# Decoding the second part's weights earlier, by way of DRAM, in a mixer and two-layer MoE kernel

## The chip, the cores and the metric

One core of a Trainium2 chip runs the whole program. The metric is device time in microseconds. The kernel before takes 967.74 us (median of 3 runs, 966.28 to 967.86). Engines are named as in the profile: PE (TensorE), DVE (VectorE), ACT (ScalarE), POOL (GpSimd), SP (the queue that issues most DMAs).

## What is computed

A linear-attention recurrence, then two feed-forward blocks on its output of 3072 rows of 384:

```
for t in range(768):                                  # 4 x 8 heads, 48 wide
    y[t] = r[t] @ (state + (u * k[t]) v[t]^T);  state = w[t] * state + k[t] v[t]^T
x = y, heads side by side                             # 3072 x 384
x = (sigmoid(x @ w_gate) * (x @ w_val)) @ w_out       # hidden 1536
h = x @ w_in                                          # hidden 2048
out = (h * tanh(log(1 + exp(h)))) @ w_out2
```

All of it is float32. The products of the feed-forward blocks are made on PE from pairs of float16 numbers (a high half and the rest), three products for each.

## The kernel before

**Pairs.** The 768 steps are cut into 24 chunks j of 32 steps, and these into 12 pairs p (0 to 11). Of each pair, `fine(p)` (L465) makes the scores inside a chunk: products on POOL into tiles `pt` and updates of the loaded block `blk` (L486), sums of `pt` on DVE into `A` (L506). `coarse(p)` (L563) turns them into operands for PE: DVE flips `RD`, `KD`, `WD` and `X`, PE makes the scores `lp` (L638), ACT and DVE merge them into `X` (L655), and three steps `scaled` (L623) multiply parts of `RD`; the last of these (768 elements) follows `lp` and stands before `yp`. `keys(p)` makes `KT` and, on ACT, `KK` (L697). `step(j)` (L706) makes the chunk's output `yp` (L728), the state's outer product `kp` (L824), its decay (L804) and its sum (L835). The output leaves as `xs` (L212, L215) and comes back transposed as `xt` by a transposing DMA that ACT issues (L762).

**First block.** For each pair 12 units `gate(p, f)` (L857): products `gv` on PE (L880), then sigmoid, product and two halves `gt` on ACT and DVE (L891 to L911). Their second product `out1(p - 1, c, part)` (L932) adds up in PSUM as `o` (L944), goes through `xo` (L212, L215) and is stored in DRAM as `x2d` (L980).

**Second block.** It begins when all pairs are done: `h_unit` (L1039) makes `h` on PE (L1054) from the weights `wis`, `operands` (L1071) sums on POOL (L1088) and halves on DVE and ACT, `out2` (L1135) multiplies by the weights `wps` (L1169). The seven products of `out2` need sums of weight blocks.

**Weights.** All weights come as 64-bit words, and are decoded to two float16 halves (`decode`, L271): a load `raw` (SP, L267), two steps on ACT (`word` L248, `low` L238), a joining step on DVE (`word`, L292), the high half (L303) and the rest (L306). For `wps`, `combine` (L314) takes the place of the last two: differences `sum_wp` (L332), then three high halves (L346) and three rests (L332). In the kernel before the second block's weights are decoded straight into `wis` and `wps`. That space is free once the attention is done (`open_a`, L1029, and `open_b`, L1035), so the 16 decodings are listed in `tail_end` (L1284), which is called at gate 7 of pair 10. Engines are given as prices: `W2HI` lets ACT or DVE make the high half, `W2LO` POOL or DVE the rest.

**Order.** Every step is a task with an engine (or several with a price each), a cost, what it reads and writes, and `lat`, the time after its end at which a follower counts as ready (`SEM`, 0.1, if nothing is said). `Plan.run` (L96) gives each task the latest time at which it may stand, from its followers, and then lists the tasks: at each step the engine that is free first takes, of the tasks that are ready, the one with the earliest latest time. PE's tasks keep their latest times in the order in which they were added. All engines then run their lists in order, SP's queue too. So a changed cost or `lat` can move any instruction.

Of the kernel before, what the change touches and what calls it, by code (L numbers as in the profile page):

```python
# [19 lines left out]
NP = NJ // 2  # L20
# [19 lines left out]
NPT = 32  # L40
NRAW = 1
YPOS = (4, 7)
SEM = 0.1
SHARED = (0,)
WHOLE = range(1, 12, 2)
COLD = 1.9
# [113 lines left out]
def mixer_moe_kernel(  # L160
# [100 lines left out]

    def load_raw(key, pool, src, n, slot, reads=()):
# [6 lines left out]
        add("sp", 2.2, go, reads, [("raw", slot)], lat=2.0)  # L269

    def decode(key, dst, n, count, slot, reads, high_on, lo_on, halves=False, blocks=None):  # L271

# [37 lines left out]
        full = 1.15 if key[0] == "wo" else 0.95  # L310
        add("act", 0.78, rebase, [raw, "consts", "table1"], [word])
        add("act", 1.1, bits3, [raw, "consts"], [low])
        add("dve", full, join, [low], [word])
        if halves:  # L314
            combine(key, dst, word, low, reads, high_on, lo_on, count)
            return
        made = [[(key[0], f, a) for f in blocks or [key[1]]] for a in range(2)]
        add(high_on, 0, high, [word, *reads], made[0])
        add(lo_on, 0, rest, [word, *made[0]], made[1])

    def combine(key, dst, word, low, reads, high_on, lo_on, count):
        sums = {}
# [28 lines left out]

        add({"pool": 1.8, "dve": 1.1}, 0, differ, [word], [low])
        for n, part in ((0, 0.25), (1, 0.5), (2, 1.0)):
            src = low if n == 2 else word
            cost = {e: c * part + 0.1 for e, c in high_on.items()}
            add(cost, 0, lambda e, n=n: high(e, n), [src, *reads], [(*key, 0, n)])
            cost = {e: c * part + 0.1 for e, c in lo_on.items()}
            add(cost, 0, lambda e, n=n: rest(e, n), [src, (*key, 0, n)], [(*key, 1, n)])

# [128 lines left out]
    def fine(p):  # L488
# [377 lines left out]
    def gate(p, f):  # L866
# [61 lines left out]
        else:  # L928
            add("act", 0.34, high, [ps], [(*G, 0), *room])
        add("dve", 0.35, rest, [ps, (*G, 0)], [(*G, 1)])  # L930
# [63 lines left out]
    def open_a(e):  # L994

        sf.close()
        w2["i"] = sb.enter_context(tc.tile_pool(name="w2i", bufs=1))
        w2["wi"] = w2["i"].tile([128, 2, KC, F2], F16, name="wis")

    def open_b(e):  # L1000
        sa.close()
        w2["p"] = sb.enter_context(tc.tile_pool(name="w2p", bufs=1, side="right"))
        w2["raw"] = sb.enter_context(tc.tile_pool(name="raw", bufs=1, side="right"))
        w2["ph"] = sb.enter_context(tc.tile_pool(name="ph", bufs=1, space=PS, side="right"))
        w2["po"] = sb.enter_context(tc.tile_pool(name="po2", bufs=1, space=PS, side="right"))
        w2["wp"] = w2["p"].tile([128, 2, 7, NF2 // 2, HD], F16, name="wps")
        w2["h"] = sb.enter_context(tc.tile_pool(name="hp", bufs=1, side="right"))

    homes = []
# [31 lines left out]
    def h_unit(r, f):  # L1041
# [3 lines left out]
        E = ("e", k)  # L1045
        fs = slice(128 * f, 128 * f + 128)

        def sums(e):
# [3 lines left out]
            for a, c in ((0, 0), (0, 1), (1, 0)):  # L1052
                for kc in range(KC):
                    nc.tensor.matmul(  # L1054
                        hps[r, f],
                        w2["wi"][:, a, kc, fs],
                        x2[r][:, c, kc, :],
# [8 lines left out]

        w = [("wi", f // 2, a) for a in range(2)]
        add("pe", 1.95, sums, [*w, ("x2", r % 2)], [ps])
# [75 lines left out]
    def out2(r, m, h):  # L1144
# [13 lines left out]
        def sums(e):  # L1158
# [8 lines left out]
            for i in range(NF2 // 2):  # L1167
                for a, c in ((0, 0), (1, 0), (0, 1)):
                    nc.tensor.matmul(  # L1169
                        ops2[h, first],  # L1170
                        home(slots[r, i, name])[:, c, tsl],
                        w2["wp"][:, a, w, i, :],
                        start=(new and n == 0),
# [22 lines left out]
        if m == 0 and h == 0:  # L1196
            add("none", 0, start, [], [O])
        n = {0: 0, 1: 1, 2: 1}.get(w, 2)
        reads = [("slot", slots[r, i, name], c) for i in range(NF2 // 2) for c in range(2)]
        reads += [("wp", i, a, n) for i in range(NF2 // 2) for a in range(2)]  # L1200
        add("pe", 1.95, sums, reads, [bank])
# [82 lines left out]
    def tail_end():  # L1284
# [3 lines left out]
        for i in range(8):  # L1288
            cs = slice(256 * i, 256 * i + 256)
            dst = lambda cs=cs: w2["wi"][:, :, :, cs]  # L1290
            load_raw(("wi", i), lambda: dp, in_cols(wi, cs), (KC, 256), i % 3)
            decode(("wi", i), dst, (KC, 256), i, i % 3, ["opened"], W2HI, W2LO)
        add("none", 0, open_b, [], ["attention", "open"])
        for i in range(8):
            cs = slice(2 * i, 2 * i + 2)
            dst = lambda i=i: w2["wp"][:, :, :, i]
            slot = (i + 2) % (3 + NRAW)
            pool = (lambda: dp) if slot < 3 else (lambda: w2["raw"])
            reads = [] if slot < 3 else ["open"]
            load_raw(("wp", i), pool, in_rows(wo2, cs), (2, DM), slot, reads)  # L1300
            decode(("wp", i), dst, (2, DM), i, slot, ["open"], W2HI, W2LO, True)

# [4 lines left out]
    for p in range(NP):  # L1307
        for f in range(NF1):
# [94 lines left out]
```

## Time and profile before

| | us |
|---|---|
| median of 3 runs | 967.74 |
| the profiled execution, its own time | 966.43 |
| its span, first to last instruction | 964.7 |
| PE busy | 895.7 |
| DVE busy | 663.6 |
| ACT busy | 496.4 |
| POOL busy | 490.7 |

The program has four stretches: a start in which the weights of the first block are decoded (0 to 160 us), the steady pairs (to about 500), a change-over in which the last pairs run while the second block's weights are decoded (to about 595), and the second block. An engine's busy time within a stretch, beside the stretch's length, tells whether it is the limit there. Idle time of PE is then looked up by what ended it.

### The profile page before, as it was taken

The numbers are of one execution on the slowest core, as the hardware profiler recorded it, in microseconds if no ns is written. First come the engines' busy times: TensorE is split into PE (matmuls) and PEld (weight loads), VectorE is DVE, ScalarE is ACT, GpSimd is POOL, SyncE is SP. The second block draws the span as 40 slices with busy tenths as digits, with TensorE's granted clock in tenths as the row PEclk, the third lists the DMA queues.
The fourth block names the chain that finished last, engine by engine and source line by source line (L and its number), as shares of the span: only waits on it lengthen the run. The fifth ranks groups of instructions, "written<-read, shape, count | busy, mean of one in ns | idle before, by whom it ended". The sixth has DMA issues, their size and how long they took to land.

```text
span 964.7 us, 29601 instructions
## 1 busy us (share of the span) xinstructions
PE 895.7 (93%) x12808; PEld 715.9 (74%) x12808; DVE 663.6 (69%) x1202; ACT 496.4 (51%) x1191; POOL 490.7 (51%) x534
## 2 busy tenths in 40 slices
PE   0667899999999999999999889999999999999998
PEld 0455678888888888888888777657767676776788
DVE  7889976767676757686778798875565655556541
ACT  2757864343525344343536566775565655656540
POOL 7999832626464545546364365654343443444330
PEclk9988899999999999999999999999999999999999
DMA  9445832322232323133223760010100102000000
GB/s 307 152 139 163 265 115 75 65 67 72 68 57 72 83 62 76 50 75 71 60 41 101 169 204 12 8 43 1 38 30 10 58 1 66 2 9 26 1 34 34
DMA packets 56467, 71.92 MB, mean 75 GB/s; under 512 B 20752, under 2 KB 37648, under 8 KB 56208
## 3 DMA queue, kind: packets, MB, share of 16 engines
q1 hardware_dynamic: 39696, 66.09, 23.6%
q10 hardware_dynamic: 16640, 3.94, 2.1%
q8 instruction: 100, 1.64, 0.7%
q14 instruction: 31, 0.25, 0.1%
HBM read 56.64 MB, written 9.44 MB: 68 GB/s over the span
## 4 chain that ended last, share of the span: by engine, by line
PE 72%; DVE 13%; ACT 7%; POOL 3%; issue 2%; ACTq 2%; DMA 1%; SPq 0%; DVEq 0%; POOLq 0%
PE gv L880 20%; PE h L1054 19%; PE o L1169 17%; PE o L944 10%; PE yp L728 3%; ACT X L655 2%; ACTq L762 2%; ACT KK L697 2%; DVE X L655 1%; DVE A L506 1%; PE lp L638 1%; POOL pt L486 1%; DVE gt L911 1%; PE kp L824 1%; DVE s L835 1%
## 5 line engine op out<-in xcount | busy, mean ns | idle before, releaser
L1054 PE MATMUL h<-x,wis 128*128 128x512 f16 x864 | 199.9, 379 | 0.0
L486 POOL TENSOR_TENSOR blk<-blk 128x384 f32<-128x384 f32 (+2 forms) x139 | 129.4, 943 | 97.6 <-DMA blk<-rkw 69.9
L880 PE MATMUL gv<-xt,wgs 128*128 128x256 f16 x1296 | 165.9, 278 | 12.3 <-DVE gt L911 11.9
L944 PE MATMUL o<-gt,wos 128*128 128x256 f16 x1296 | 165.2, 273 | 5.9 <-DVE xo L215 5.9
L1088 POOL TENSOR_TENSOR sum<-e 128x256 f32<-128x256 f32 x96 | 71.5, 744 | 186.3 <-ACT e L1065 186.2
L880 PE MATMUL gv<-xt,wvs 128*128 128x256 f16 x1296 | 163.6, 276 | 2.5 <-DVE wvs L306 1.2
L880 PEld LDWEIGHTS <-wgs 128*128 128x128 f16 x1296 | 126.3, 100 | 31.4 <-issue 12.9
L1054 PEld LDWEIGHTS <-wis 128*128 128x128 f16 x864 | 83.5, 98 | 82.9
L944 PEld LDWEIGHTS <-wos 128*128 128x128 f16 x1296 | 126.0, 98 | 24.5 <-issue 6.8
L880 PEld LDWEIGHTS <-wvs 128*128 128x128 f16 x1296 | 125.0, 99 | 20.9 <-DVE wvs L306 1.5
L486 POOL TENSOR_TENSOR pt<-blk 128x384 f32<-128x384 f32 x93 | 105.4, 1157 | 47.0 <-DMA blk<-rkw 43.6
L891 ACT ACTIVATE sig<-gv 128x256 f32<-128x256 f32 x144 | 53.5, 385 | 118.2 <-PE gv L880 114.3
L1065 ACT ACTIVATE e<-h 128x512 f32<-128x512 f32 x96 | 57.2, 596 | 84.6 <-PE h L1054 83.7
L911 DVE TENSOR_TENSOR gt<-gv,gt 128x256 f16<-128x256 f32 x144 | 58.8, 417 | 51.6 <-ACT gt L908 50.1
L908 ACT CAST gt<-gv 128x256 f16<-128x256 f32 x144 | 52.6, 371 | 75.9 <-DVE gv L896 55.3
L896 DVE SCALAR_TENSOR_TENSOR gv<-gv,sig 128x256 f32<-128x256 f32 x144 | 60.7, 431 | 29.3 <-ACT sig L891 28.8
L1169 PE MATMUL o<-wps,gt 128*128 128x192 f16 x612 | 74.0, 246 | 0.0
L655 ACT COPY X<-lp 24x64 f32<-24x64 f32 x174 | 44.5, 256 | 38.2 <-DVE X L655 28.1
L1107 DVE SCALAR_TENSOR_TENSOR gt<-e,gt 128x256 f16<-128x256 f32 x41 | 27.3, 675 | 49.6 <-ACT gt L1102 49.6
L506 DVE TENSOR_REDUCE A<-pt 128x32 f32<-128x768 f32 (+1 forms) x60 | 51.4, 863 | 12.3 <-POOL pt L486 12.3
L1169 PE MATMUL o<-wps,wgs 128*128 128x192 f16 x498 | 59.4, 246 | 0.0
L1169 PE MATMUL o<-wps,wos 128*128 128x192 f16 x456 | 57.1, 246 | 0.0
(106 smaller groups left out, 1508.4 us busy)
## 6 DMA issues: line engine op xcount, KB each, us to landing
v<-vt SPq DMA_DIRECT2D x96, 96.0 KB, 3.3
blk<-rkw SPq DMA_DIRECT2D x22, 384.0 KB, 3.5
raw_wi<-wi SPq DMA_DIRECT2D x8, 768.0 KB, 4.8
raw_wp<-wo SPq DMA_DIRECT2D x8, 768.0 KB, 6.2
blk<-rkw SPq DMA_DIRECT2D x11, 512.0 KB, 4.0
raw_wg<-wg SPq DMA_DIRECT2D x6, 768.0 KB, 6.2
raw_wv<-wv SPq DMA_DIRECT2D x6, 768.0 KB, 6.1
raw_wo<-wo SPq DMA_DIRECT2D x6, 768.0 KB, 4.7
```

The source lines that it names most:

```text
L486: engines[e].tensor_tensor(out=pv, in0=a, in1=b, op=ALU.mult)
L506: nc.vector.tensor_reduce(out=cell(), in_=shape(pts.pop(n)), op=ALU.add, axis=AX.X)
L655: put(out=xp[p][rs, xs, t:], in_=lps[p, e][rs, :, c : c + C - t])
L880: nc.tensor.matmul(gps[p, f][:, o], w[:, a, kc, fs], xt[p][:, c, kc, :], start=(n == 0), stop=(n == 3 * KC - 1),)
L891: nc.scalar.activation(out=sgs[p, f], in_=gps[p, f][:, 0], func=AF.Sigmoid, scale=1.0 / (SW * SX))
L896: nc.vector.scalar_tensor_tensor(out=gps[p, f][:, 1], in0=gps[p, f][:, 1], scalar=SG / (SW * SX), in1=sgs.pop((p, f)), op0=ALU.mult, op1=A ...
L911: nc.vector.tensor_tensor(out=gt[p][:, 1, f], in0=gps[p, f][:, 1], in1=gt[p][:, 0, f], op=ALU.subtract,)
L944: nc.tensor.matmul(ops[p, c][:, :NT], wos[:, a, f, cs], gt[p][:, g, f, :], start=(f == 0 and n == 0), stop=(f == NF1 - 1 and n == 2),)
L1054: nc.tensor.matmul(hps[r, f], w2["wi"][:, a, kc, fs], x2[r][:, c, kc, :], start=(n == 0), stop=(n == 3 * KC - 1),)
L1065: nc.scalar.activation(out=es[r, f], in_=hps[r, f], func=AF.Mish, scale=ih)
L1088: engines[e].tensor_tensor(out=sums[0][:, n - 1], in0=a(), in1=b(), op=op)
L1169: nc.tensor.matmul(ops2[h, first], home(slots[r, i, name])[:, c, tsl], w2["wp"][:, a, w, i, :], start=(new and n == 0), stop=(n == 3 * NF2 ...
```

## The change

**Decoding ahead.** `decode_ahead` is new. It decodes one of the 16 pieces (8 of `wi`, 8 of `wp`) into a staging tile in the first block's own buffer `raw2`, and stores it in DRAM (`wid`, `wpd`). `ahead(n, tick)` lists it after gate unit f of pair p where 12 (p - 3) + f = 5 n + 2, that is from pair 3 gate 2 to pair 9 gate 5; its load reads that gate's "tick". Its tasks have `lat` 3.0 (`SLACK`) in place of 0.1, its load 9.0. High halves are ACT's alone, rests and differences POOL's alone. `tail_end` now holds only loads of finished weights from DRAM (`fetch`), 8 of 384 KB into `wis` and 8 of 672 KB into `wps`, whose layouts have the piece as the first index after the partition.

**Planner.** The scores' products of pairs 3 and later have `lat` 1.5 (`EASY`) and the step that multiplies by `U` is priced 1.7 in place of 1.2.

**PSUM.** `out1` of pairs 10 and 11 takes banks "po2" and "po" in turn; before, only pair 11's second one had "po2".

```
-W2HI = {"act": 0.83, "dve": 0.7}
-W2LO = {"pool": 1.65, "dve": 0.92}
+W2HI = {"act": 0.83}
+W2LO = {"pool": 1.65}
...
+    wid = dram.tile([8, 128, 2, KC, 256], F16, name="wid")
+    wpd = dram.tile([8, 128, 2, 7, HD], F16, name="wpd")
...
-        add({"pool": 1.8, "dve": 1.1}, 0, differ, [word], [low])
+        add("pool", 2.4, differ, [word], [low], lat)
...
+    def decode_ahead(name, i, src, n, made, store, tick):
+        key = (name, i)
+        count = 8 * (name == "wp") + i
+        slot = count % 2
+        stage = ("raw", 2)
...
+        add("none", 0, new, [], [stage])
+        load_raw(key, lambda: dp, src, n, slot, [tick], 3 * SLACK)
+        decode(
+            key, lambda: tiles[0], n, count, slot, [stage], W2HI, W2LO, name == "wp", None, SLACK
+        )
...
+        add(
+            "sp",
+            0.6,
+            lambda e: nc.sync.dma_start(out=store[i], in_=tiles[0]),
+            [*parts, stage],
+            [(name, "stored", i)],
+            lat=2.0,
+        )
...
-            attn(both, 0, go, [R, K], [pt])
+            wait = SEM if p < 3 else EASY
+            attn(both, 0, go, [R, K], [pt], wait)
             if scaled:
-                attn("dve", 1.2, times_u, ["U"], [pt])
+                attn("dve", 1.7, times_u, ["U"], [pt])
...
-        last = p == NP - 1
-        bank = "po2" if last and c == 1 else "po"
+        bank = "po2" if p > NP - 3 and (KC * p + c) % 2 else "po"
...
+    def fetch(name, src, i, opened):
+        def go(e):
+            nc.sync.dma_start(out=w2[name][:, i], in_=src[i])
+        made = [(name, i)]
+        add("sp", 0.6, go, [(name, "stored", i), opened], made, lat=2.5)
...
         for i in range(8):
-            cs = slice(256 * i, 256 * i + 256)
-            dst = lambda cs=cs: w2["wi"][:, :, :, cs]
-            load_raw(("wi", i), lambda: dp, in_cols(wi, cs), (KC, 256), i % 3)
-            decode(("wi", i), dst, (KC, 256), i, i % 3, ["opened"], W2HI, W2LO)
+            fetch("wi", wid, i, "opened")
         add("none", 0, open_b, [], ["attention", "open"])
         for i in range(8):
+            fetch("wp", wpd, i, "open")
...
+            n, rem = divmod(NF1 * (p - AHEAD) + f, 5)
+            if rem == 2 and 0 <= n < 16:
+                ahead(n, ("tick", p, f))
```

The order of PE is the same from pair 3 on but for a few units that change places with a neighbour. Three places show what moved. The first is DVE while PE works at gates 1 to 4 of pair 11 (`gv11_1` to `gv11_4`; `xo` is what PE's `o` waits for). Before:

```order
L911 TENSOR_TENSOR gt11_9399<-gv11_2_9404,gt11_9399 128x256
L292 SCALAR_TENSOR_TENSOR word_wp4_9365<-word_wp4_9365,low_wp4_9442 128x768
L346 CAST wps_9219<-word_wp4_9365 128x192
L346 CAST wps_9219<-word_wp4_9365 128x2x192
L896 SCALAR_TENSOR_TENSOR gv11_3_9444<-gv11_3_9444,sig_9501 128x256
L215 SCALAR_TENSOR_TENSOR xo_9515<-o110_0_9389,xo_9515 128x256
L332 TENSOR_TENSOR wps_9219<-word_wp4_9365,wps_9219 128x2x192
L292 SCALAR_TENSOR_TENSOR word_wp5_9498<-word_wp5_9498,low_wp5_9520 128x768
L911 TENSOR_TENSOR gt11_9399<-gv11_3_9444,gt11_9399 128x256
```

The same gates on DVE after the change:

```order
L953 TENSOR_TENSOR gt11_9525<-gv11_2_9531,gt11_9525 128x256
L938 SCALAR_TENSOR_TENSOR gv11_3_9561<-gv11_3_9561,sig_9603 128x256
L953 TENSOR_TENSOR gt11_9525<-gv11_3_9561,gt11_9525 128x256
L219 SCALAR_TENSOR_TENSOR xo_9617<-o110_0_9515,xo_9617 128x256
L938 SCALAR_TENSOR_TENSOR gv11_4_9606<-gv11_4_9606,sig_9650 128x256
```

No decoding is left on DVE there; its last joining step stands in pair 10's first gate. The second place is POOL in the steady pairs, where the block of pair 7 comes in. Before:

```order
L623 TENSOR_TENSOR RD6_4452<-RD6_4452,WD6_4478 128x32x16
L486 TENSOR_TENSOR blk6_2990<-blk6_2990 128x2x8x24
L804 TENSOR_TENSOR s13_4379<-s12_4187,WD6_4478 128x384
L486 TENSOR_TENSOR blk6_2990<-blk6_2990 128x24
L486 TENSOR_TENSOR blk6_2990<-blk6_2990 128x16x24
L486 TENSOR_TENSOR pt_4659<-blk7_3831 128x768
L486 TENSOR_TENSOR pt_4689<-blk7_3831 128x384
L486 TENSOR_TENSOR blk7_3831<-blk7_3831 128x16x24 x2
```

The same place on POOL after the change (`made_wi3` is a rest; `RD6` of 32x24 is the last `scaled`, on which `yp` waits):

```order
L527 TENSOR_TENSOR blk6_3022<-blk6_3022 128x16x24
L846 TENSOR_TENSOR s13_4391<-s12_4191,WD6_4493 128x384
L527 TENSOR_TENSOR pt_4722<-blk7_3851 128x768
L527 TENSOR_TENSOR pt_4745<-blk7_3851 128x384
L310 TENSOR_TENSOR made_wi3_4585<-word_wi3_4461,made_wi3_4585 128x768
L665 TENSOR_TENSOR RD6_4465<-RD6_4465,WD6_4493 128x32x24
L527 TENSOR_TENSOR blk7_3851<-blk7_3851 128x16x24 x2
L527 TENSOR_TENSOR pt_5120<-blk7_3851 128x8x48 x2
```

The last `scaled` has come over from DVE (in pairs 4 to 8 and 10; in pair 11 it went from POOL to DVE), behind a rest. The third place is SP's queue at the change-over. Before:

```order
L980 DMA x2d_86<-xo_8520 128x512
L267 DMA raw_wi5_8645<-wi 128x3x512
L267 DMA raw_wi6_8674<-wi 128x3x512
L980 DMA x2d_86<-xo_8747 128x512
L267 DMA raw_wi7_8804<-wi 128x3x512
L267 DMA raw_wp0_8926<-wo2 128x2x768
L267 DMA raw_wp2_8994<-wo2 128x2x768
L267 DMA raw_wp3_9026<-wo2 128x2x768
L267 DMA raw_wp4_9122<-wo2 128x2x768
```

SP's queue at the change-over after the change:

```order
L395 DMA wpd_88<-made_wp6_8590 128x2688
L1051 DMA wis_8843<-wid_87 128x1536 x8
L1021 DMA x2d_86<-xo_8976 128x512
L1021 DMA x2d_86<-xo_9290 128x512
L395 DMA wpd_88<-made_wp7_8856 128x2688
L1080 DMA x2_0_9369<-x2d_86 128x3x256 x4
L1080 DMA x2_1_9401<-x2d_86 128x3x256 x4
L1051 DMA wps_9365<-wpd_88 128x2688 x7
```

The eight loads of raw words have become one run of eight loads of `wis` and, behind the loads of `x2`, one of `wps`.

## Rows read from the trace of the kernel before

**Rows 1.** The page: busy time, share of the span and instructions of each engine.
```profile
PE 895.7 (93%) x12808; PEld 715.9 (74%) x12808; DVE 663.6 (69%) x1202; ACT 496.4 (51%) x1191; POOL 490.7 (51%) x534
```

**Rows 2.** Stretches: length; busy PE, PEld, DVE, ACT, POOL; clock, DMA share, GB/s.
```profile
60.00:160.00 100.00, 82.78 (x1559) 68.38 (x1557) 83.63 (x145) 72.44 (x153) 65.64 (x58) 0.90 0.51 158
160.00:500.00 340.00, 336.69 (x6574) 290.87 (x6572) 239.24 (x453) 140.15 (x399) 177.49 (x185) 1.00 0.28 66
...
520.00:590.00 70.00, 62.24 (x943) 53.44 (x941) 59.26 (x101) 44.63 (x90) 37.61 (x36) 1.00 0.60 163
590.00:930.00 340.00, 340.00 (x2684) 237.03 (x2683) 206.35 (x395) 197.65 (x461) 148.62 (x193) 1.00 0.07 23
```

**Rows 3.** Waits of PE from 500 to 600: us in total, times, longest.
```profile
PE o L944 <- DVE xo L215: 4.3, 3, 2.3
PE gv L880 <- issue: 1.6, 2, 1.2
PE yp L728 <- issue: 1.4, 2, 0.7
PE yp L728 <- DVE s L835: 0.5, 2, 0.3
```

**Rows 4.** Stretches between PE's four waits on "issue", columns as in rows 2.
```profile
528.45:533.55 5.10, 3.91 (x128) 3.10 (x128) 4.19 (x10) 4.01 (x11) 0.90 (x1) 1.00 0.49 153
533.55:540.75 7.20, 6.00 (x126) 4.79 (x127) 7.17 (x9) 4.16 (x7) 2.39 (x2) 1.00 0.87 173
540.75:545.88 5.13, 4.70 (x128) 3.90 (x128) 4.10 (x5) 3.57 (x8) 1.64 (x1) 1.00 0.94 259
```

**Rows 5.** The page: the queue that brings PE's instructions; packets, MB, share.
```profile
q8 instruction: 100, 1.64, 0.7%
```

**Rows 6.** The page: DMA issues, with count, KB each and us to landing.
```profile
blk<-rkw SPq DMA_DIRECT2D x22, 384.0 KB, 3.5
raw_wi<-wi SPq DMA_DIRECT2D x8, 768.0 KB, 4.8
```

**Rows 7.** Waits of PE from 160 to 500, columns as in rows 3.
```profile
PE yp L728 <- DVE RD L623: 1.8, 3, 0.7
PE yp L728 <- DVE s L835: 1.3, 4, 0.6
```

**Rows 8.** DVE's joining steps from 510 to 592: busy us, mean ns, idle before.
```profile
L292 DVE SCALAR_TENSOR_TENSOR word_wp<-word_wp,low_wp 128x768 uint32<-128x768 uint32 x8 | 8.4, 1047 | 0.9 <-ACT low_wp L238 0.9
```

**Rows 9.** POOL's groups from 510 to 592, columns as in rows 8.
```profile
L332 POOL TENSOR_TENSOR sum_wp<-word_wp,sum_wp 128x192 f32<-128x192 f32 x14 | 10.5, 753 | 1.1
L306 POOL TENSOR_TENSOR wis<-word_wi,wis 128x768 f16<-128x768 f32 x6 | 10.1, 1684 | 19.8 <-DVE wis L303 14.7 <-ACT wis L303 5.1
L332 POOL TENSOR_TENSOR sum_wp<-word_wp 128x384 f32<-128x384 f32 x8 | 8.9, 1116 | 13.1 <-DVE word_wp L292 13.1
L332 POOL TENSOR_TENSOR wps<-sum_wp,wps 128x768 f16<-128x768 f32 x3 | 5.5, 1818 | 0.9 <-ACT wps L346 0.9
...
L623 POOL TENSOR_TENSOR RD<-RD,WD 128x768 f32<-128x768 f32 x1 | 1.5, 1486 | 0.5 <-PE lp L638 0.5
```

**Rows 10.** Line L623 on DVE, 200 to 500: ns min/median/max, first and last start.
```profile
L623 DVE TENSOR_TENSOR RD<-RD,WD x7: 946/949/1597, 217.9 to 482.3; 128x768 f32<-128x768 f32 x7
```

**Rows 11.** PE in order of time, from a pair's last `lp` to `yp`: start, us.
```profile
215.91 0.88 PE L638 MATMUL lp<-RD,KD 64*32 64x48 f32 x64
216.73 2.14 PE L880 MATMUL gv<-xt,wvs 128*128 128x256 f16 x18
...
218.95 0.29 PE L728 MATMUL yp<-s,RD 64*32 64x48 f32 x8
```

**Rows 12.** Waits of PE from 60 to 160, columns as in rows 3.
```profile
PE gv L880 <- DVE gt L911: 11.9, 4, 4.0
PE xp L747 <- ACT xs L212: 2.2, 1, 2.2
...
PE gv L880 <- DVE wvs L306: 1.2, 1, 1.2
```

More of the change, by code (lines that the diff above doesn't have):

```diff
@@ L40 @@
 NPT = 32
-NRAW = 1
 YPOS = (4, 7)
@@ L44 @@
 SHARED = (0,)
+AHEAD = 3
+SLACK = 3.0
+EASY = 1.5
 WHOLE = range(1, 12, 2)
@@ L260, in next_pg, with load_raw @@
         return ("pg", npg[0] % n)
-    def load_raw(key, pool, src, n, slot, reads=()):
+    def load_raw(key, pool, src, n, slot, reads=(), lat=2.0):
         def go(e):
@@ L267, in go, with decode @@
             nc.sync.dma_start(out=raws[key], in_=src)
-        add("sp", 2.2, go, reads, [("raw", slot)], lat=2.0)
-    def decode(key, dst, n, count, slot, reads, high_on, lo_on, halves=False, blocks=None):
+        add("sp", 2.2, go, reads, [("raw", slot)], lat=lat)
+    def decode(key, dst, n, count, slot, reads, high_on, lo_on, halves=False, blocks=None, lat=SEM):
         raw = ("raw", slot)
@@ L310, in decode, with combine @@
         full = 1.15 if key[0] == "wo" else 0.95
-        add("act", 0.78, rebase, [raw, "consts", "table1"], [word])
-        add("act", 1.1, bits3, [raw, "consts"], [low])
-        add("dve", full, join, [low], [word])
+        add("act", 0.78, rebase, [raw, "consts", "table1"], [word], lat)
+        add("act", 1.1, bits3, [raw, "consts"], [low], lat)
+        add("dve", full, join, [low], [word], lat)
         if halves:
-            combine(key, dst, word, low, reads, high_on, lo_on, count)
+            combine(key, dst, word, low, reads, high_on, lo_on, count, lat)
             return
         made = [[(key[0], f, a) for f in blocks or [key[1]]] for a in range(2)]
-        add(high_on, 0, high, [word, *reads], made[0])
-        add(lo_on, 0, rest, [word, *made[0]], made[1])
-    def combine(key, dst, word, low, reads, high_on, lo_on, count):
+        add(high_on, 0, high, [word, *reads], made[0], lat)
+        add(lo_on, 0, rest, [word, *made[0], *reads], made[1], lat)
+    def combine(key, dst, word, low, reads, high_on, lo_on, count, lat):
         sums = {}
@@ L355, in combine, with new @@
             cost = {e: c * part + 0.1 for e, c in high_on.items()}
-            add(cost, 0, lambda e, n=n: high(e, n), [src, *reads], [(*key, 0, n)])
+            add(cost, 0, lambda e, n=n: high(e, n), [src, *reads], [(*key, 0, n)], lat)
             cost = {e: c * part + 0.1 for e, c in lo_on.items()}
-            add(cost, 0, lambda e, n=n: rest(e, n), [src, (*key, 0, n)], [(*key, 1, n)])
+            add(cost, 0, lambda e, n=n: rest(e, n), [src, (*key, 0, n), *reads], [(*key, 1, n)], lat)
+    def decode_ahead(name, i, src, n, made, store, tick):
[3 more added lines that the diff above has]
+        stage = ("raw", 2)
+        tiles = []
+        def new(e):
+            t = dp.tile([128, 3072], F16, tag="raw2", name=f"made_{name}{i}")
+            size = 2
+            for k in made:
+                size *= k
+            names = "abcd"[: len(made) + 1]
+            dims = {x: k for x, k in zip(names, (2, *made))}
+            tiles.append(
+                t[:, :size].rearrange(f"p ({' '.join(names)}) -> p {' '.join(names)}", **dims)
+            )
[4 more added lines that the diff above has]
+        )
+        if name == "wp":
+            parts = [(*key, a, k) for a in range(2) for k in range(3)]
+        else:
+            parts = [(*key, a) for a in range(2)]
+        add(
[5 more added lines that the diff above has]
+            lat=2.0,
+        )
     def decode_early(name, i, dst, src, count):
@@ L929, in gate @@
             add("act", 0.34, high, [ps], [(*G, 0), *room])
-        add("dve", 0.35, rest, [ps, (*G, 0)], [(*G, 1)])
+        add("dve", 0.35, rest, [ps, (*G, 0)], [(*G, 1), ("tick", p, f)])
     def out1(p, c, part):
-        last = p == NP - 1
-        bank = "po2" if last and c == 1 else "po"
+        bank = "po2" if p > NP - 3 and (KC * p + c) % 2 else "po"
         cs = slice(128 * c, 128 * c + 128)
@@ L1045, in h_unit @@
         E = ("e", k)
-        fs = slice(128 * f, 128 * f + 128)
+        fs = slice(128 * (f % 2), 128 * (f % 2) + 128)
         def sums(e):
@@ L1055, in sums @@
                         hps[r, f],
-                        w2["wi"][:, a, kc, fs],
+                        w2["wi"][:, f // 2, a, kc, fs],
                         x2[r][:, c, kc, :],
@@ L1065, in unit @@
             nc.scalar.activation(out=es[r, f], in_=hps[r, f], func=AF.Mish, scale=ih)
-        w = [("wi", f // 2, a) for a in range(2)]
+        w = [("wi", f // 2)]
         add("pe", 1.95, sums, [*w, ("x2", r % 2)], [ps])
@@ L1197, in out2 @@
             add("none", 0, start, [], [O])
-        n = {0: 0, 1: 1, 2: 1}.get(w, 2)
         reads = [("slot", slots[r, i, name], c) for i in range(NF2 // 2) for c in range(2)]
-        reads += [("wp", i, a, n) for i in range(NF2 // 2) for a in range(2)]
+        reads += [("wp", i) for i in range(NF2 // 2)]
         add("pe", 1.95, sums, reads, [bank])
@@ L1288, in tail_end, with ahead @@
         for i in range(8):
-            cs = slice(256 * i, 256 * i + 256)
-            dst = lambda cs=cs: w2["wi"][:, :, :, cs]
-            load_raw(("wi", i), lambda: dp, in_cols(wi, cs), (KC, 256), i % 3)
-            decode(("wi", i), dst, (KC, 256), i, i % 3, ["opened"], W2HI, W2LO)
+            fetch("wi", wid, i, "opened")
         add("none", 0, open_b, [], ["attention", "open"])
         for i in range(8):
-            cs = slice(2 * i, 2 * i + 2)
[L1296 to L1301, printed above, removed]
+            fetch("wp", wpd, i, "open")
+    def ahead(n, tick):
+        i = n % 8
+        if n < 8:
+            cs = slice(256 * i, 256 * i + 256)
+            decode_ahead("wi", i, in_cols(wi, cs), (KC, 256), (KC, 256), wid, tick)
+        else:
+            cs = slice(2 * i, 2 * i + 2)
+            decode_ahead("wp", i, in_rows(wo2, cs), (2, DM), (7, HD), wpd, tick)
     cells = {0: fine(0)}
```

7 lines of the change are left out of this document (3 added, 4 removed).

## The prediction

> **The bound now.** I read the page's busy times first: PE is busy for 895.7 of 964.7 us [rows 1], so the most that any change of the other engines' work can bring is PE's idle time, and the question is where that lies and who ends it. The stretches answer the first half [rows 2]. From 590 to 930 PE never idles (340.00 of 340.00), and its order there is unchanged. In the steady pairs, 160 to 500, it idles 3.3 us of 340, with DVE at 70%, POOL at 52% and ACT at 41%. From 520 to 590 it idles 7.8 us of 70, with DVE at 85% and a DMA share of 0.60: this is where the second block's weights are decoded. From 60 to 160 it idles 17.2 us at a granted clock of 0.90. The waits answer the second half. At the change-over [rows 3] they add up to 7.8 us: 4.3 for `xo` on DVE, 3.0 on "issue" in four pieces (1.6 and 1.4), 0.5 for the state's sum.
>
> "Issue" means that nothing the profile shows ended the wait, so I looked at what lies between the four. From the end of one to the end of the next PE starts 128 matmuls and 128 weight loads, or 126 and 127 [rows 4], some 256 instructions each time. The queue that brings PE's instructions carried 1.64 MB in 100 packets [rows 5] for 25,616 matmuls and weight loads [rows 1], 256 each. So these are waits of PE for its next packet of instructions, while the data queues are at a share of 0.49 to 0.94. In the steady pairs, at a share of 0.28 [rows 2], the list of PE's waits has only the two rows of rows 7, and neither is of this kind.
>
> [...]
>
> **The change-over.** All 16 decodings leave it. DVE keeps only gates, `xo`, `xs` and the attention's last steps, and `out1` gets a second bank, so that `o` need not wait until `xo` has emptied the first. I take the whole 4.3 us; the other bound is 2.9, if one of the three stays at its mean of 1.4. The 0.5 us for the state's sum I leave as it is (bound: gone).
>
> Of the instruction waits some stay. The raw loads become eight loads of 384 KB in one run, which start once the last pair's scores are made and their space is free, and eight of 672 KB after the attention. A raw load of 768 KB lands in 4.8 us [rows 6]; the first run is four times as much, so at most 19 us, over about half of the four places. Half of 3.0 goes: 1.5 (bounds 0 and 3.0). The second run falls where PE works at gates of 256 columns, with few instructions in a microsecond, and ends long before `out2` needs it. Sum for the change-over: 4.3 + 1.5 = 5.8 us less (bounds 2.9 and 7.8).
>
> **Steady pairs.** A pair takes (482.3 - 217.9) / 6 = 44.1 us [rows 10]. What comes in:
>
> DVE: 16 joining steps at 1.05 us [rows 8], 17 us, less six `scaled` of 0.95 [rows 10]. On 239 of 340 busy that is hidden by DVE's idle third; without that cover it would be 11 us.
>
> ACT: even if all of its 44.6 us from 520 to 590 moved, it would be busy 185 of 340 [rows 2]: hidden.
>
> POOL: a rest of `wi` takes 1.68. A piece of `wp` takes 1.12 + 2 x 0.75 for the differences, and 1.82 for the largest rest; with the other two in proportion to their size (a quarter and a half) 3.2, together 5.8 (an estimate from rows 9). Eight of each are 60 us. The worst pairs hold 12 / 5 = 2.4 pieces of `wp`, 14 us, on 177.5 / 340 x 44.1 = 23 us [rows 2], plus 1.5 for `scaled`: 38.5 of 44.1. POOL does not become the bound, though only 5.6 us are left in such a pair.
>
> The last `scaled`: from the end of `lp` (215.91 + 0.88) to the first matmul that reads it (218.95) lie 2.16 us [rows 11]. DVE needs 0.95 and still made PE wait three times, 1.8 us in all [rows 7, 10]. On POOL it takes 1.49 [rows 9] and leaves 0.67; a rest of 1.68 that has just begun in front of it makes PE wait 1.0. In six pairs that is between 0 and 6.0, against today's 1.8, so between -1.8 and +4.2. I take two waits of 1.0 and 0.3 for the others, 2.3 against 1.8, so +0.5: in two of the six (pairs 5 and 6) the row just ahead on POOL is a full rest, in two more a small step of a decoding, in two a product of the scores.
>
> Instruction waits: 16 loads of 768 KB and 16 stores are new there. Loads of 384 KB run there today without such waits [rows 6, 7]; one of twice that size may cost one wait of 3.0 / 4 = 0.75 [rows 3]. Bounds 0 and 16 x 0.75 = 12; I take 1.0, near the row of the steady pairs, since these loads come one at a time and not five in a row.
>
> SP's queue also carries the 32 transfers, and waits in order for POOL's rests before each store; the loads of `v` and `blk` behind it are issued a pair ahead, and I give that nothing (bound 1).
>
> **The start.** Two joining steps and six ACT steps for `wi` leave it, and changed due times change the order between 80 and 125 us. On DVE the last rest of `wvs` goes to POOL, which takes the wait of 1.2 away, and one `gt` is put ahead of the flip of `X`, which shortens one of the four waits of 11.9 [rows 12]. Against that, ACT's `xs` of the fourth chunk now stands behind two decoding steps, which lengthens the wait of 2.2. I take 1.0 less; bounds 1.2 + 11.9 / 4 = 4.2 less, and 3.0 more, another such wait.
>
> **Sum.** -5.8 + 0.5 + 1.0 - 1.0 = -5.3. The profiled execution took 966.43, so 961.1; it lies 1.3 under the median of 967.74, so the forecast is 962.4.
>
> **Rivals.** (a) Slower: the instruction waits move into the steady pairs. If each of the 16 raw loads brings one wait of 0.75, these cost 12 in place of 1.0: 962.4 + 11 = 973.4. For it speaks that loads of this size stood by all four waits [rows 4, 6]; against it, that today's loads cause none in 340 us. It decides from 6.3 / 0.75, nine waits on, since without this term the sum is -6.3. Chance 0.11.
>
> (b) No difference: POOL's rests hold up the recurrence. Each of six `scaled` late by 1.0 and the state's decay, which is also moved to POOL in some pairs, as late as `s` is now (1.3 more [rows 7]): 4.2 - 0.5 + 1.3 = 5.0 above the forecast, 967.4. For it speaks how DVE's `scaled` grew from 0.95 to 1.60 [rows 10], and that rests now stand ahead of it; against it, POOL's 5 us to spare. Chance 0.15. [...]
>
> (c) More: all of the 7.8 goes, the start gains 4.2, no new wait comes: 967.7 - 12 - 1.8 = 954, more likely some part of it, 956. Chance 0.07.
>
> That the decodings stay where they were is ruled out by the order on DVE.
>
> **The numbers.** The forecast has 0.67; by its own bounds it lies between 958.5 and 965.6. For a range that holds 8 in 10 I reach up over (b) to 969.5 and down to 957; what is left out is (a) and most of (c), some 0.17. A measurement of this kernel tells 0.2%, 1.9 us, from no change. Faster by more than that is the forecast and (c), 0.74; within it (b), 0.15; slower (a), 0.11.
>
> **The test.** Right: PE idle from 520 to 590 under 3 us, no wait for `xo` there, DVE under 50 us busy in it; at most one or two waits on "issue". The steady pairs should stay within 2 us of their idle 3.3. Wrong: waits on "issue" spread over 160 to 500, 256 instructions apart (a); `yp` waiting for POOL's `RD` in most pairs (b); waits for `gt`, which would mean that ACT or DVE is held up somewhere I priced at nothing; or a start that is over 3 us longer.

## The result, and the profile after

The changed kernel takes 978.54 us (median of four runs) where the kernel before takes 967.01 beside it: a ratio of 1.0126, 95% interval 1.0113 to 1.0138. It is 11.5 us slower. The forecast was 962.4, and the range ended at 969.5.

The page's busy times after, to be set beside [rows 1]:

```profile
PE 899.7 (92%) x12808; PEld 718.9 (74%) x12808; DVE 632.8 (65%) x1157; ACT 505.0 (52%) x1213; POOL 516.8 (53%) x557
```

DVE has 31 us less to do and POOL 26 more. PE is busy 4.0 us longer with the same 12,808 matmuls; the rest of its longer span is idle time. To see where, I cut the span at the start of the third pair's first gate, of the ninth pair's first gate, and of the first `h` (the program counts pairs from 0, so the third pair is its pair 2). The columns are those of [rows 2]; first the kernel before:

```profile
0.00:155.84 155.84, 102.12 (x2036) 83.62 (x2037) 131.60 (x206) 98.10 (x204) 117.07 (x110) 0.93 0.58 184
155.84:421.05 265.21, 262.03 (x5019) 226.63 (x5016) 187.84 (x355) 107.50 (x308) 136.06 (x143) 1.00 0.28 66
421.05:596.70 175.65, 166.81 (x2770) 144.31 (x2768) 135.56 (x237) 91.08 (x216) 90.59 (x90) 1.00 0.36 96
596.70:961.45 364.75, 364.75 (x2990) 261.36 (x2987) 208.26 (x404) 199.68 (x466) 147.03 (x192) 1.00 0.07 24
```

and the changed kernel, cut at the same four places of the program:

```profile
0.00:159.43 159.43, 101.96 (x2037) 83.22 (x2038) 131.32 (x198) 97.54 (x212) 114.34 (x107) 0.86 0.50 155
159.43:437.37 277.94, 266.14 (x5019) 229.22 (x5017) 190.24 (x364) 127.75 (x325) 165.15 (x163) 0.98 0.41 111
437.37:609.06 171.69, 166.82 (x2771) 145.08 (x2768) 104.19 (x196) 81.26 (x215) 90.26 (x96) 0.99 0.48 144
609.06:973.81 364.75, 364.75 (x2990) 261.37 (x2987) 206.65 (x401) 198.50 (x462) 147.05 (x192) 1.00 0.07 24
```

- The start takes 3.6 more, all of it idle time of PE (length less busy: 53.7, then 57.5).
- The steady pairs three to eight take 12.7 more: idle 3.2, then 11.8; and PE's same work takes 266.1 in place of 262.0, at a clock of 0.98 in place of 1.00.
- The change-over takes 4.0 less: idle 8.8, then 4.9.
- From the first `h` on nothing differs.

So most of the gain that I forecast at the change-over came, and the steady pairs, where I held the new work to be hidden, cost three times as much. PE's waits there, from 160 to 500 (columns of [rows 3], and to be set against [rows 7]):

```profile
PE o L985 <- DVE xo L219: 4.7, 3, 2.3
PE kp L866 <- DVE X L697: 3.0, 1, 3.0
PE yp L770 <- issue: 1.5, 2, 1.1
PE o L985 <- issue: 1.0, 1, 1.0
PE yp L770 <- DVE RD L665: 0.6, 1, 0.6
PE kp L866 <- issue: 0.5, 1, 0.5
```

None is for POOL. The waits for `xo` and `X` are new, and so are the four on issue. From 500 to 600 there is one row of any size, where [rows 3] had `xo` and issue:

```profile
PE o L985 <- DVE xo L219: 4.0, 2, 3.0
```

What makes `xo` late is seen around the second of those waits, of 2.08 us, which ends at 313.70. DVE in order of time (start, us, and in brackets the idle time before and who ended it):

```profile
304.54 0.90 DVE L697 COPY X<-lp 24x64 f32<-24x64 f32 x3 [0.92 <-PE lp L680]
306.40 0.93 DVE L697 COPY X<-lp 24x64 f32<-24x64 f32 x3 [0.95 <-ACT X L697]
307.36 0.96 DVE L527 TENSOR_TENSOR pt<-pt,U 128x768 f32<-128x768 f32 x1
310.41 0.92 DVE L697 COPY X<-lp 24x64 f32<-24x64 f32 x3 [2.09 <-ACT X L697]
312.23 0.96 DVE L697 COPY X<-lp 24x64 f32<-24x64 f32 x3 [0.90 <-ACT X L697]
313.22 0.42 DVE L219 SCALAR_TENSOR_TENSOR xo<-o,xo 128x256 f16<-128x256 f32 x1
```

and ACT beside it:

```profile
307.37 0.84 ACT L697 COPY X<-lp 24x64 f32<-24x64 f32 x3 [1.00 <-DVE X L697]
308.23 0.38 ACT L216 ACTIVATE xo<-o 128x256 f16<-128x256 f32 x1
...
308.76 0.91 ACT L252 ACTIVATE word_wi<-raw_wi 128x768 f32<-128x768 f32 x1
309.57 0.81 ACT L697 COPY X<-lp 24x64 f32<-24x64 f32 x3
311.37 0.83 ACT L697 COPY X<-lp 24x64 f32<-24x64 f32 x3 [0.99 <-DVE X L697]
```

The scores of a pair are merged into `X` in eight sets, four from each of two PSUM banks. A set is three copies (`x3` in the lines). The planner holds the sets to be independent and deals them out to ACT and DVE. In the trace the sets of one bank go strictly one after another: each waits for the one before it, on the other engine. The chain lasts from 304.5 to 313.2, with a decoding step (`word_wi`) inside it; DVE is tied to it and idle for almost half of it, and the second half of `xo`, whose first half is done at 308.6, stands behind its last link. In the kernel before the chain was there too, but `xo` stood ahead of it:

```profile
300.90 0.41 DVE L215 SCALAR_TENSOR_TENSOR xo<-o,xo 128x256 f16<-128x256 f32 x1
302.16 0.92 DVE L655 COPY X<-lp 24x64 f32<-24x64 f32 x3 [0.84 <-ACT X L655]
303.97 0.96 DVE L655 COPY X<-lp 24x64 f32<-24x64 f32 x3 [0.90 <-ACT X L655]
```

The 4.1 us of longer busy time stand behind two of the waits; in the other stretches from 159 to 437 the granted clock is 1.00. The stretches shown are the ten us after a wait of 2.3, then a wait of 3.0 and the ten us after it; the clock is the third number from the end:

```profile
361.00:371.00 10.00, 10.00 (x244) 8.05 (x242) 5.18 (x13) 5.22 (x12) 5.35 (x6) 0.83 0.42 104
...
407.00:410.00 3.00, 0.05 (x2) 0.03 (x1) 1.85 (x7) 1.93 (x8) 0.00 (x0) 0.83 0.00 0
410.00:420.00 10.00, 10.00 (x229) 7.94 (x230) 6.69 (x15) 4.83 (x10) 3.17 (x3) 0.71 0.61 182
```

The mean clock changes from one execution to the next: over the four of the changed kernel it went from 0.970 (the profiled one) to 0.984, and the times differ by 1.5 us.

### The profile page after: what moved, and what is told of

Read it like the earlier page. It is cut to its first block, busy times and chain, and to the rows that moved or that the text cites. A ratio compares the mean times of both kernels' runs of the same rounds, so it can differ in the third digit from the quotient of the medians.

```text
span 977.1 us, 29683 instructions
## 1 busy us (share of the span) xinstructions
PE 899.7 (92%) x12808; PEld 718.9 (74%) x12808; DVE 632.8 (65%) x1157; ACT 505.0 (52%) x1213; POOL 516.8 (53%) x557
## 5 line engine op out<-in xcount | busy, mean ns | idle before, releaser
L985 PE MATMUL o<-gt,wos 128*128 128x256 f16 x1296 | 168.7, 276 | 13.8 <-DVE xo L219 8.7
L527 POOL TENSOR_TENSOR pt<-blk 128x384 f32<-128x384 f32 x93 | 112.7, 1236 | 28.0 <-DMA blk<-rkw 22.0
L739 ACT COPY KK<-KT 32x384 f32<-32x384 f32 x96 | 48.9, 509 | 17.7 <-DVE KT L730 14.4
```

Of the source, the lines that this page charges most:

```text
L527: engines[e].tensor_tensor(out=pv, in0=a, in1=b, op=ALU.mult)
L739: nc.scalar.copy(out=whole, in_=own)
L985: nc.tensor.matmul(ops[p, c][:, :NT], wos[:, a, f, cs], gt[p][:, g, f, :], start=(f == 0 and n == 0), stop=(f == NF1 - 1 and n == 2),)
```

## The experiments

Times are medians, each beside runs of the kernel before on the same chip (966.0 to 966.6; 967.0 beside the changed kernel), with the ratio to it. Where I set two of these kernels against each other, the difference of their medians is good to about 1 us, by which the kernel before itself differs between these sets. "Steady" is the stretch from the third pair's first gate to the ninth's, as above: 265.2 with 3.2 idle before, 277.9 with 11.8 idle after. Its row is shown for each kernel on which a verdict rests, with the columns of [rows 2].

**The second bank alone**, in the kernel before.

```
-        bank = "po2" if last and c == 1 else "po"
+        bank = "po2" if p > NP - 3 and (KC * p + c) % 2 else "po"
```

> The kernel before, with only the second bank for every other `o` of the last two pairs. By my prediction the three waits of `o` for `xo` at the change-over (4.3 us) hang on the single bank: 2.9 to 4.3 less, about 963. The rival: in the changed kernel `xo` itself comes late on DVE, and `o` still waits 4.0 us there; if a late `xo` is what counts and not the bank, at most 1 us less, about 966.

965.65, ratio 0.9995 (0.9976 to 1.0014): no difference. Its waits from 520 to 620:

```profile
PE gv L880 <- issue: 2.3, 1, 2.3
PE o L943 <- DVE xo L215: 1.4, 1, 1.4
PE h L1053 <- DVE gt L911: 1.3, 1, 1.3
PE gv L880 <- DVE gt L911: 1.1, 1, 1.1
```

The wait for `xo` shrinks from 4.3 to 1.4 as I had bounded it, but waits of 2.4 for `gt` take its place: DVE is as loaded there as before (busy 59.7 us from 520 to 590, 59.3 before). So the bank by itself saves nothing that can be measured; what the change-over saved came with the rest of the change.

**The two planner numbers alone**, in the kernel before.

```
-            attn(both, 0, go, [R, K], [pt])
+            wait = SEM if p < 3 else 1.5
+            attn(both, 0, go, [R, K], [pt], wait)
...
-                attn("dve", 1.2, times_u, ["U"], [pt])
+                attn("dve", 1.7, times_u, ["U"], [pt])
```

> The kernel before, with only the two planner numbers for the fine scores changed (0.5 us more for the product with `U`, 1.5 us between products and sums from the fourth pair on). Up to 125 us its order is nearly that of the changed kernel. If these numbers alone cost what the start lost (+3.6 us at the third pair's first gate; POOL works at the fourth pair's products while `o` waits 4.0 us for a rest of `wos`, then PE runs at a clock of 0.69), this takes 3 to 5 us more than before, about 971, and has both waits. The rival: the start is late because of the decoding steps that were moved; then no difference, 967.

970.66, ratio 1.0042 (1.0028 to 1.0056). The numbers alone cost 4.4 us, and the third pair begins 2.7 later than before. Its largest waits from 60 to 160 are:

```profile
PE gv L881 <- DVE gt L912: 12.7, 6, 4.4
PE o L945 <- POOL wos L306: 5.2, 2, 3.8
```

The wait for `wos` is that of the changed kernel, where POOL's queue reads:

```profile
115.63 2.67 POOL L527 TENSOR_TENSOR pt<-blk 128x384 f32<-128x384 f32 x2
118.26 1.64 POOL L310 TENSOR_TENSOR wos<-word_wo,wos 128x768 f16<-128x768 f32 x1
```

while PE waits from 115.92 to 119.95: products of the fourth pair, due earlier by the new numbers, are ahead of a rest that `o` needs. So the start's loss comes with the numbers and not with the decoding steps that left it. (Kernels further down with the same numbers in another order start earlier than the kernel before; it is the order that these numbers led to here.)

**No change of engine, banks side by side.** The changed kernel in its own order, but one bank's merges on DVE, the other's on ACT.

```
-... lambda on, e=e, n=n: merge(on, e, n), ...
+... lambda on, e=e, n=n: merge(("dve", "act")[e], e, n), ...
```

> The changed kernel in the same order, but the merges of `X` of one bank all on DVE and those of the other all on ACT, in place of a choice set by set. Hand-over theory: the merges of a bank go strictly one after another, each change of engine makes DVE or ACT stand still, and `xo`, `gt` and `kp` behind them come late; with no change of engine the waits for `xo` (4.7 us from 160 to 520, 4.0 at the change-over) and for `X` (3.4) mostly go: 6 to 10 us less than the changed kernel, about 970. The rival: the decoding steps' own time on DVE and ACT makes `xo` late; then within 2 us of 978.5.

963.15, ratio 0.9965 (0.9949 to 0.9980): 15.4 us less than the changed kernel, and faster than the kernel before.

```profile
158.73:422.16 263.43, 261.02 (x5019) 226.38 (x5016) 192.91 (x367) 127.89 (x322) 165.76 (x164) 1.00 0.42 117
```

Steady idle is 2.4, less than before the change, with all the decoding in it. DVE at the seventh pair is through with its four sets 3.8 us after the first begins, and `xo` follows behind one product:

```profile
303.24 3.80 DVE L697 COPY X<-lp 24x64 f32<-24x64 f32 x12 [0.92 <-PE lp L680]
...
308.50 0.42 DVE L219 SCALAR_TENSOR_TENSOR xo<-o,xo 128x256 f16<-128x256 f32 x1
```

**No arithmetic of the decodings**, order and transfers as in the changed kernel: rebasing, joining, halves and differences are planned as before, and issue nothing.

```
+    def quiet(eng, cost, fn, reads, writes, lat):
+        plan.add(eng, cost, lambda e: None, reads, writes, lat)
...
+        add = quiet if lat == SLACK else plan.add
```

> The changed kernel in the same order without the arithmetic of the sixteen decodings (their loads, stores and later loads stay; zeros are stored, so the second block's part of the output is nothing). If the decoding steps on ACT, DVE and POOL make the steady pairs late, most of their 12 to 14 us goes: about 967. If hand-overs between ACT and DVE do it by themselves, or the other order, 3 to 6 us go: about 974. If the waits for instructions beside the loads do it, nearly nothing goes: 977.

972.8, ratio 1.0069 (1.0048 to 1.0091).

```profile
161.38:433.25 271.87, 261.68 (x5018) 226.59 (x5016) 178.09 (x353) 102.40 (x289) 139.92 (x146) 1.00 0.42 114
```

5.7 us come back, and 10.2 of idle time (3.9 of it on issue) stay in the steady stretch though no arithmetic of a decoding is left on any engine: the order that was planned around it is enough for most of the idle time. What does go in the profiled execution is the low clock (busy 261.7, not 266.1); at 970.73 us that execution is the fastest of six, so how much of this the others share is not shown.

**Change of engine in the order of before**, set by set, last set on DVE.

```
-... lambda on, e=e, n=n: merge(on, e, n), ...
+... lambda on, e=e, n=n: merge(("act", "dve")[n % 2], e, n), ...
```

> The kernel before in its own order, with the merges of `X` turned into a strict change of engine from set to set (ACT, DVE, ACT, DVE in each bank, the last on DVE); nothing is decoded ahead. If change of engine in itself makes `xo` and `gt` late, as in the changed kernel's fifth to ninth pairs, this loses 5 to 15 us against before: about 975, with waits for `xo` and `X` from 160 to 500. If it takes the decoding steps between the sets to do so, within 3 us of before: 967 to 969.

965.8, ratio 0.9995 (0.9977 to 1.0012), steady idle 1.6:

```profile
155.08:418.64 263.56, 261.93 (x5018) 226.62 (x5016) 192.07 (x372) 102.17 (x288) 135.66 (x143) 1.00 0.27 67
```

At the seventh pair the alternating sets run from 299.33, the first one on ACT, to 307.10, the last one on DVE:

```profile
299.33 0.83 ACT L655 COPY X<-lp 24x64 f32<-24x64 f32 x3 [0.20 <-PE lp L638]
...
306.14 0.96 DVE L655 COPY X<-lp 24x64 f32<-24x64 f32 x3 [0.90 <-ACT X L655]
```

A chain of 7.8 us, not much shorter than the 8.7 of the changed kernel, loses nothing in the order of before. **The split in the order of before** is the control:

> The kernel before in its own order, with the merges of one bank on DVE and of the other on ACT. Its steady pairs have 3.3 us of idle time to give, the change-over 4.3 for `xo`: 0 to 4 us less than before, about 964. If the gain of the split in the changed kernel (15.4 us) came from something other than the late `xo` and `X`, such as less work per set, it shows here too: 955.

965.13, ratio 0.9982 (0.9968 to 0.9996), steady idle 3.9. The split is worth little there.

**`xo` ahead**, the rest of the changed kernel's order as it was: both halves, and they alone, are issued where the planner holds what they need to be done (`soon` is set for these tasks alone).

```
+        if not self.soon:
+            return self.begin
+        return min(self.begin, max(d.end for d in self.deps))
```

> The changed kernel in the same order but for `xo`: its two halves are issued on ACT and DVE where the planner holds their bank to be full, ahead of the merges of the second bank that stood before them. The merges change engine as in the changed kernel and the decoding steps stay between them. If the place of `xo` behind those merges is what cost the steady pairs, the waits for `xo` (4.7 us from 160 to 520, 4.0 at the change-over) go and 6 to 10 us come back: about 970, close to the split kernel but for waits of `kp` for `X`. If the load on DVE and ACT is what counts, the work behind `xo` is late in its place, in waits for `gt` and `X`: 976 to 979.

976.58, ratio 1.0106 (1.0084 to 1.0127): only 2 us come back, and my theory on the place of `xo` falls. Its steady row, and its waits from 160 to 500:

```profile
158.41:434.98 276.57, 267.10 (x5019) 229.75 (x5017) 191.23 (x364) 128.11 (x325) 166.65 (x163) 0.98 0.40 112
```

```profile
PE o L991 <- issue: 3.5, 2, 2.0
PE kp L872 <- DVE X L703: 2.6, 1, 2.6
PE gv L928 <- DVE gt L959: 1.5, 1, 1.5
PE yp L776 <- DVE s L883: 1.4, 2, 1.2
```

The wait for `xo` is gone, but `gt`, `s` and `X` itself are waited for instead, and the waits on issue stay (3.5 from 160 to 500, after 3.0): what stands behind the chain is late as a whole, not one step of it. So what spares the alternating sets in the order of before is not the place of `xo` alone either.

**One engine for all eight sets**, order as in the changed kernel. This separates the changes of engine from the time for which an engine is tied. First all on DVE; the other kernel has "act" in its place.

```
-... lambda on, e=e, n=n: merge(on, e, n), ...
+... lambda on, e=e, n=n: merge("dve", e, n), ...
```

> The changed kernel in the same order, all eight sets of merges on DVE: no change of engine, but DVE is tied from the first set to the last. If the changes of engine cost the time, it goes as in the split kernel: 962 to 967. If it is the time for which an engine with the gates' steps behind it is tied to the merges, DVE's eight sets of 0.93 (7.4 us from first to last, against 8.4 in the changed kernel's seventh pair) leave `xo` and `gt` nearly as late: 973 to 978.

989.3, ratio 1.0239 (1.0224 to 1.0255).

```profile
166.35:442.08 275.73, 262.60 (x5019) 227.21 (x5016) 211.35 (x439) 109.84 (x250) 164.81 (x163) 0.99 0.42 112
```

> The changed kernel in the same order, all eight sets of merges on ACT: again no change of engine; DVE is free, ACT is tied for 8 x 0.83 = 6.6 us, with sigmoids and the first halves of `gt` and `xo` behind or between. If the changes of engine cost the time: 962 to 967. If the tied time does: between the split kernel and the all-DVE one, 966 to 974.

974.68, ratio 1.0083 (1.0063 to 1.0103).

```profile
158.35:432.73 274.38, 265.83 (x5018) 229.05 (x5016) 173.82 (x295) 145.95 (x394) 166.27 (x164) 0.98 0.41 113
```

Without a single change of engine the steady idle is 13.1 with DVE tied and 8.6 with ACT tied, against 2.4 with the banks side by side. So the loss needs no change of engine, and in the order of before eight alternating sets cause none. The length of the chain doesn't do it by itself either: 7.8 us go with 1.6 of steady idle in the order of before. What is left is both together: this order queues the gates' steps behind sets that run in series, and the split, in the same order, ties each engine for less than half the chain. DVE is the worse one to tie. The 10.8 us by which the all-DVE kernel is slower than the changed one don't lie in the steady pairs, which take 2.2 less (more idle, but a higher clock): its start takes 6.9 more and its change-over 5.1. I had set it at 978 at most and left both out.

**The planner told the truth**: the changed kernel, planned anew with merges out of one bank in series.

```
-attn(..., [banks[e]], [X[e][n]])
+attn(..., [banks[e]], [X[e][n], ("row", *banks[e])])
```

> The changed kernel planned anew with one thing more told to the planner: merges out of one bank go one after another, on whichever engine. If the loss came from a plan that held them to be parallel, the plan now puts `xo` ahead of them itself, the waits for `xo` and `X` from 160 to 590 go, and the time comes near that of the split kernel: 960 to 968. If a new plan only moves the loss: 972 or more.

963.26, ratio 0.9976 (0.9959 to 0.9993), steady idle 4.2.

```profile
153.84:419.74 265.90, 261.70 (x5019) 226.40 (x5016) 189.48 (x349) 133.13 (x340) 167.24 (x166) 1.00 0.41 116
```

The waits for `xo` are gone from the steady pairs; at the seventh pair the plan now puts `xo` (299.33 on DVE) ahead of all eight sets by itself. Against the kernel before it is a small gain; against the changed kernel it is 15 us. In the profiled executions the steady pairs take 12.0 less than in the changed kernel, and the start 5.6. Other new plans moved the time too (by 4.4 with the two numbers alone), so a few of the 15 may be due to the new order and not to what the planner was told. **Planned with the split**:

```
-attn({"act": 0.82, "dve": 0.93}, 0, ...)
+attn({"act": 0.82} if e else {"dve": 0.93}, 0, ...)
```

> The changed kernel planned anew with the merges of one bank on DVE and of the other on ACT (the split kernel has the changed kernel's order). Same theory: waits for `xo` and `X` gone, 958 to 966. If the gain of the split kernel hung on the old order as well: over 968.

960.84, ratio 0.9943 (0.9924 to 0.9963), steady idle 4.0.

**The old numbers under each of these plans** (product with `U` at 1.2, the 1.5 us from the fifth pair on).

> The kernel told of merges in series, planned with the old number for the product with `U` and with the 1.5 us between products and sums only from the fifth pair on. If those two numbers cost the start 4 us, as in the kernel before with the two numbers (970.66 against 966.22), this takes 3 to 5 us less than the serial kernel and its third pair begins 3 to 5 us earlier. If only the order that they led to in those kernels cost it, within 2 us of the serial kernel either way.

962.48, ratio 0.9966 (0.9954 to 0.9977); the third pair begins 0.3 us later than in the serial kernel.

> The kernel planned with the merges of one bank on DVE and the other on ACT, now with the old number for the product with `U` and the 1.5 us between products and sums only from the fifth pair on. Its third pair's rests of `wos` are due earlier. If these numbers cost anything by themselves, 2 to 4 us less than 960.8; if only an order does, as the serial kernels showed, within 2 us of it.

959.63, ratio 0.9923 (0.9903 to 0.9944), the best of the kernels that compute the whole output; its third pair begins 0.7 us earlier than in the kernel planned with the split. Its steady pairs idle 6.6 us, more than before the change: what it gains over the kernel before lies in the start (5.3) and the change-over (5.7). Both are within 2 us of their partners, so the numbers by themselves cost about a microsecond at most; the orders that they led to cost more. **The same numbers on the split kernel in its old plan**:

> The split kernel, planned with the old number for the product with `U`, and with the 1.5 us between products and sums only from the fifth pair on. The last rests of `wos` then stand ahead of the fourth pair's products on POOL. If the planner's numbers cost what the start lost, the waits for `wos` and most of the wait for `gt` at 127 go, and with them the low clock from 120 to 140: 3 to 6 us less than the split kernel, about 959. If the start is late for another reason, or the other order costs the steady pairs as much: 962 to 965.

966.7, ratio 0.9998 (0.9978 to 1.0018): 3.6 slower than the split kernel. The wait for `wos` is gone and the third pair begins 1.0 earlier, but other waits came at the start, and the new order loses again in the steady pairs (265.9, idle 4.1). My 959 was wrong.

**Without the transfers**: the split kernel with fourteen of the raw loads and fourteen of the stores taken out.

> The split kernel without fourteen of the sixteen raw loads and of the sixteen stores (all steps of the decodings stay and work on the first two pieces, and the first stored piece is loaded later, so the second block's part of the output is wrong). If the waits on issue of the split kernel (1.8 from 160 to 520, 1.1 at the change-over) hang on these transfers: 2 to 4 us less than the split kernel, about 960. If such waits come from the program alone: within 1 us of it, 963.

959.38, ratio 0.9927 (0.9904 to 0.9950): 3.8 less than the split kernel. In the trace 1.5 of that is there at the start of the third pair already, before these loads begin. Steady waits on issue are 0.9 against 1.2, and from there to the first `h` 1.9 against 1.7. So the time came out where the first theory put it, but by luck: the transfers that were taken out don't account for the waits on issue. What does stays open.

## Why the prediction was wrong, point by point

- **Steady pairs, DVE and ACT "hidden".** This is the step that failed. I compared busy time with idle time (a third of DVE idle, so 11 us are hidden, and all of ACT's), as if a free engine were free for any step. The order decides that: in the changed plan, eight sets that the planner took for parallel, and that ran in series, stood ahead of `xo`, `gt` and `s`, so PE waited 7.7 us for `xo` and `X`. Priced at nothing, the step cost 12.7 us with the rest: 8.6 of idle time (3.0 of waits on issue are in it, and earlier waits went) and 4.1 of lower clock in the profiled execution. Split by bank in the same order, the same work left 2.4 us of idle time.
- **POOL and rival (b).** No wait for a `scaled` of POOL occurs; `yp` waits 0.6 for one of DVE. The term of +0.5 was, with the waits of 3.1 in [rows 7] nearly gone, about -2.5.
- **Instruction waits, rival (a).** Four in the steady pairs, 3.0 us where I took 1.0, within the bounds. Two of them, at 322.20 and 326.30, are 127 matmuls and 128 weight loads apart, as in [rows 4]. Between the others lie 2038 and 1786, within a few of eight and seven times 256. But 10,036 matmuls and weight loads run in the steady stretch, some 39 times 256, and only four waits on issue came: most stretches of 256 pass without one. That these are waits for a packet of instructions was my reading of such counts; no run shows what ends them. Nine were needed for (a), and they didn't come.
- **The change-over.** -4.0 where I had -5.8, within the bounds, by other pieces than I named: all waits on issue went (I kept half), and `xo` is still waited for 4.0 us (I took all of it away, and the second bank for the cause).
- **The start.** +3.6 where I took -1.0, above the bound of +3.0. I weighed single steps of the new order, and missed that POOL's rest of `wos` now stood behind the fourth pair's products (4.0), an order that the two planner numbers led to.
- **The tests that I named.** DVE is busy 34.5 us from 520 to 590, under 50, but PE idles 4.5, not under 3, and `xo` is waited for. The steady idle rose by 8.6 where I allowed 2, and the start was 3.6 longer. Those two signs were named, and waits for `gt` as a sign of an engine held up somewhere that I priced at nothing; the waits that came, for `xo` and `X` in the steady pairs, were in none of my rivals.
- **Numbers that were wrong in themselves.** DVE's joining steps were priced at 1.05 us from [rows 8], which hold only the eight of `wp`; six of `wi` in the same stretch took 1.46 each. The sixteen took 21.4 us after the change where I had 17 (19.4 before it). And "by its own bounds" the forecast doesn't lie between 958.5 and 965.6: the bounds given for the terms, added up, reach from 13.8 less to 17.3 more, about 954 to 985. The measured time lies inside those, and outside the range that I gave.

Whether the sets of one bank could run side by side is not shown. In the traces of the two kernels they go one after another (DVE is idle for 0.95, 2.09 and 0.90 us, until ACT's set ends, before three of its sets in the lines of the changed kernel above), and no run takes those waits away.

## What to carry to other kernels

When work is put into an engine's idle time, ask which steps are queued behind it and who waits for them; a share of idle time answers neither. Where a planner sets the order, compare what it holds to be parallel with what the trace shows to be in series, before pricing any change that makes it plan anew. Then tell it: the kernel planned with one more dependency was 15 us faster here, more than the change was meant to bring.

## What the runs showed of the hardware that I had not expected

- The same wait is not always followed by a lower clock. A wait of 2.3 us for `xo` ends at 360.4 in the changed kernel and at 360.6 in the one without the decodings' arithmetic. In the stretch from 360 to 370 the clock is 0.83 in the first and 1.00 in the second. Each is one execution, and why they differ is open.
- DVE's joining step has no one price: in the traces of the kernel before and of the changed one it takes from 0.93 to 2.40 us. Its length goes with whether POOL is inside an instruction when it begins. If so, the step lasts until that instruction ends and about 0.81 us more, but no less than about 0.93; if not, 0.93 to 0.96 (twelve steps), even when POOL begins one meanwhile (in four of them). Each of the two traces holds 28 such steps (128x768), and 55 of these 56 fit within 0.03 us. In the other one, at 57.64 in the changed kernel, POOL's instruction had begun less than 0.01 us before, and DVE's step took 0.95. The first two lines are the longest step of the kernel before and the POOL instruction that was under way; the last is a step of the changed kernel with no POOL instruction beside it:

```profile
540.84 1.64 POOL L306 TENSOR_TENSOR wis<-word_wi,wis 128x768 f16<-128x768 f32 x1 [3.02 <-DVE wis L303]
540.89 2.40 DVE L292 SCALAR_TENSOR_TENSOR word_wi<-word_wi,low_wi 128x768 uint32<-128x768 uint32 x1
...
316.54 0.95 DVE L296 SCALAR_TENSOR_TENSOR word_wi<-word_wi,low_wi 128x768 uint32<-128x768 uint32 x1
```
